# A new written issue order for an attention and feed-forward kernel on one core

## The chip, the core and the metric

The kernel runs on one core of a Trainium2 chip. A core has five engines, each with an instruction queue of its own that is worked off strictly in order: TensorE (PE; its weight loads are shown apart as PEld), VectorE (DVE), ScalarE (ACT), GpSimd (POOL) and SyncE (SP), which here only issues transfers. An instruction at the head of a queue that waits for another engine or for a transfer holds up everything behind it on that queue. The metric is the device time of one execution in microseconds (us).

## The reference

Causal-window attention with eight global keys, four sequences of 768 tokens, eight heads of 64; its output, 3072 x 512, goes through a feed-forward layer of 2048 with softplus in between:

```python
scores = scale * np.matmul(q, k.transpose(0, 1, 3, 2))
keep = is_global | is_local                      # the first 8 keys, and the last 96
scores = np.where(keep, scores + bias[None], -1000000000.0)
a = np.exp(scores - np.max(scores, axis=-1, keepdims=True))
a = a / (np.sum(a, axis=-1, keepdims=True) + 1e-09)
x = np.matmul(a, v)                              # then (B, S, H * D)
h = x @ w_in
g = np.maximum(h, 0.0) + np.log1p(np.exp(-np.abs(h)))
out = g @ w_out
```

The bias is minus a slope of the head times the distance; with only the last 96 and the first 8 keys kept, a block of 128 queries needs its own block of keys, the one before it, and the global keys, which are copied into unused rows of the block before.

## The kernel before, in words

**Tiling.** The 24 blocks of 128 queries (n = 0 to 23) are loaded in 12 units of two blocks. Two blocks make a group (g = 0 to 11) of 256 tokens for the feed-forward part. All of w_in and w_out stays on the chip in bf16. q, k, v and both weights arrive in float32 in a ring of 12 buffers (`raw`) and are cast to bf16 by DVE, ACT or POOL; a buffer is loaded again only when its casts are done.

**Operations.** Each step is an `op` with a name, and the names are what the order and this text speak of:

- `ldq`, `ldk`, `ldv` (lines 573 and 583): a unit's loads, 512 KB, for the first three units' q and k in two halves of 256 KB. `win0` to `win7` and `wout0` to `wout7` (614): the weights, 512 KB each.
- `castq`, `castk`, `castv` (634, 658): casts of a unit; `castv0.11` is unit 0, block 1, second half of the rows. `cin`, `cout` (616): casts of the weights.
- `trq`, `trk`: q and k transposed, for units 0 to 2 on PE (721) with the eviction `cpq`, `cpk` (728), later by a transposing transfer on SP (741).
- `sb`, `sc` (783 to 846): scores, for blocks 0 and 1 with the bias added by PE; for the others DVE adds it (`z`, 872). `ex` (806, 879): the exponential on ACT.
- `gk`, `gv` (754, 764): copies of the global keys and values into the block before.
- `pv` (898): probabilities times values, two halves of the heads; a column of ones gives the sums. `nm` (909, 910): a reciprocal and a multiplication on DVE.
- `xt`: the block transposed, for blocks 0 to 5 on PE (929) with the copy `xc` (934), later by a transfer on SP (941).
- `a{g}.{p}` (956): eight matmuls, 256 of the 2048 hidden columns of a group into one of two PSUM banks; p = 0 and 1 need `cin0` and `cin1`, p = 6 and 7 need `cin6` and `cin7`. `e` (971): exp on ACT. `ln` (982): log(1 + e) of two `a` steps at once.
- `b{g}.{ns}.{x}` (1003) for groups 0 to 2: products with w_out, and the eviction `oc` (1032). From group 3 on the product of the 2x2 blocks is made with seven multiplications in place of eight: `ws` (defined from line 391: sums of w_out blocks, done once), `ka{g}.{j}` (447: differences of the blocks of g), `b{g}.{j}` (512: eight matmuls), `oe` (477 to 498: the seven products put together). `st` (1035, 548): stores.
- `fill` (1116): 35 matmuls on a blank tile, on PE only; nothing reads them.

**Order and engines.** `Program` (from line 21) records every `op` with what it reads and writes. The string `ORDER` (lines 68 to 148) names all 1061 operations once, each with a letter for its engine; `PLACED` (149) splits it. `Program.op` takes the engine of an operation from there, and `in_order` issues the operations in the order of the string, after it has seen that every producer stands before its consumer. The string thus fixes each engine's queue completely, and, for those operations that may run on several engines, the engine:

```python
o.eng = self.placed[name]
...
for name in self.placed:
    o = self.ops[name]
    assert all(d.name in done for d in o.deps), (name, [d.name for d in o.deps if d.name not in done])
```

Waits between engines follow from reads and writes. Beyond those, the loads of units 3 to 11 wait for a given `a` step (`gates`), and the fillers follow each other. The numbers for durations and ranks in the calls of `op` play no part once the string is there.

Of the kernel before, what the change touches and what calls it, by code (L numbers as in the profile page):

```python
# [1271 lines left out]
```

## Time and profile before

| | us |
|---|---|
| median of 3 runs (lowest, highest) | 213.37 (212.76, 213.74) |
| the profiled execution | 213.29 |
| its span, first to last instruction | 211.4 |
| PE busy in it | 202.0 |
| ACT busy | 179.3 |
| DVE busy | 161.0 |
| POOL busy | 106.9 |
| granted TensorE clock, mean | 1.000 |

The views used: the page (busy time of each engine, groups of instructions by source line), the waits of an engine (who waited for whom: us in total, times, longest), the chain of work that ended last, the timeline (start, duration, engine, line, operation, what is written from what, and in brackets the idle time before it and what ended it), and the table of stretches (busy time of each engine between two moments). Rows are by source line; since both kernels issue each engine's operations in the order of the string, the n-th instruction of an engine is known by its name, and the texts below use the names.

By stage: until 19 us PE mostly runs fillers and the attention of the first blocks; from 24 us on it is busy nearly all the time; the last matmul of the program starts near 208, and four stores end the span. The 16 transfer engines are busy all the time until about 43 us (q, k, v of three units and both weights), and again in most of the time from 55 to 160.

### The profile page before, as it was taken

To read this page: it belongs to the slowest core of one execution; us is meant where nothing else is said; L and a number is where in the kernel's file an instruction comes from. 1 tells how busy PE (TensorE), PEld (TensorE's weight loads), DVE (VectorE), ACT (ScalarE), POOL (GpSimd) and SP (SyncE) were. 2 spreads that over 40 slices of the span, in tenths; PEclk is the share of its full clock that TensorE was granted. 3 is DMA by queue.
4 is the path that set the end of the run, shared out by engine and by line. 5 is a ranking of instruction groups with operands and counts; after the bars stand their busy time and mean duration, and the time that the engine had idled before them with its cause. 6 is when DMAs were issued, how large, how long until landed. Compare 5 with 4: busy or idle time off the path is not lost.

```text
span 211.4 us, 5443 instructions
## 1 busy us (share of the span) xinstructions
PE 202.0 (96%) x2176; PEld 161.8 (77%) x2187; DVE 161.0 (76%) x292; ACT 179.3 (85%) x260; POOL 106.9 (51%) x130
## 2 busy tenths in 40 slices
PE   7987999999999988999999999999999999999994
PEld 2564786666765766988988889889889889988883
DVE  4665888888779976988798898786868989624554
ACT  6886999999998899888899989998999899877510
POOL 4466541618769463565038794564465436061070
PEclk9999999999999999999999999999999999999999
DMA  5999999949996899976399988777595510300413
GB/s 202 348 329 321 395 387 353 333 119 211 290 225 154 206 256 177 323 187 126 103 232 185 242 213 175 175 181 174 134 210 130 179 22 3 101 3 0 152 77 122
DMA packets 69848, 40.98 MB, mean 194 GB/s; under 512 B 30144, under 2 KB 61376, under 8 KB 69824
## 3 DMA queue, kind: packets, MB, share of 16 engines
q1 hardware_dynamic: 69392, 39.99, 71.4%
q10 hardware_dynamic: 432, 0.66, 0.9%
q8 instruction: 17, 0.28, 0.6%
q14 instruction: 7, 0.06, 0.1%
HBM read 27.26 MB, written 6.29 MB: 159 GB/s over the span
## 4 chain that ended last, share of the span: by engine, by line
PE 64%; ACT 14%; DMA 11%; SPq 3%; issue 3%; POOL 2%; DVE 2%; DVEq 0%; POOLq 0%
PE h_ps L956 29%; PE o_ps L512 22%; DMA raw<-in_moe_w_out_dram 5%; ACT e L971 4%; PE s_ps L846 4%; DMA raw<-in_moe_w_in_dram 4%; PE x_ps L898 3%; PE o_ps L1003 3%; ACT g L982 3%; ACT pb L879 3%; DMA raw<-in_q_dram 3%; SPq L573 2%; PE x_ps L512 2%; POOL w_out_bf L616 1%; PE s_ps L512 1%
## 5 line engine op out<-in xcount | busy, mean ns | idle before, releaser
L956 PE MATMUL h_ps<-XT,w_in_bf 128*128 128x256 bf16 x768 | 94.5, 273 | 2.4 <-ACT XT L934 1.4
L956 PEld LDWEIGHTS <-w_in_bf 128*128 128x128 bf16 x768 | 72.9, 98 | 13.5 <-issue 1.2
L971 ACT ACTIVATE e<-h_ps 128x512 f32<-128x512 f32 x96 | 58.3, 635 | 11.4 <-PE h_ps L956 11.1
L982 ACT ACTIVATE g<-e 128x1024 bf16<-128x1024 f32 x48 | 49.8, 1056 | 0.8
L872 DVE TENSOR_TENSOR z<-s_ps,biasA 128x1024 f32<-128x1024 f32 x38 | 45.8, 1218 | 4.7 <-PE s_ps L846 2.6
L879 ACT ACTIVATE pb<-z 128x1024 bf16<-128x1024 f32 (+1 forms) x44 | 43.2, 993 | 0.2
L512 PEld LDWEIGHTS <-g 128*128 128x128 bf16 x288 | 27.6, 98 | 3.2
L658 POOL CAST kb<-raw 64x512 bf16<-64x512 f32 x25 | 17.1, 682 | 23.6 <-DMA raw<-in_k_dram 11.0
L447 POOL TENSOR_TENSOR g<-g 128x1024 bf16<-128x1024 bf16 x7 | 15.3, 2187 | 19.3 <-DVE raw L447 17.2
L658 POOL CAST vb<-raw 64x512 bf16<-64x512 f32 x30 | 19.2, 641 | 7.2 <-DMA raw<-in_v_dram 5.8
L512 PEld LDWEIGHTS <-raw 128*128 128x128 bf16 x216 | 20.7, 98 | 2.5
L764 POOL COPY vb<-vb 4x512 bf16<-4x512 bf16 x19 | 12.1, 638 | 19.0 <-PE x_ps L898 18.6
L512 PE MATMUL o_ps<-raw,raw 128*128 128x256 bf16 x168 | 20.8, 273 | 0.0
L898 PEld LDWEIGHTS <-pb 128*128 128x128 bf16 x352 | 16.6, 97 | 4.9 <-ACT pb L879 0.9
L447 DVE TENSOR_TENSOR raw<-g 128x1024 bf16<-128x1024 bf16 x21 | 15.1, 729 | 4.5 <-PE s_ps L512 2.4
L910 DVE TENSOR_TENSOR xs<-x_ps,rcp 128x256 bf16<-128x256 f32 x40 | 17.0, 425 | 1.4
L512 PE MATMUL o_ps<-raw,g 128*128 128x256 bf16 x144 | 18.0, 273 | 0.0
L447 POOL TENSOR_TENSOR raw<-g 128x1024 bf16<-128x1024 bf16 x6 | 13.1, 2184 | 7.8 <-ACT g L982 7.6
L898 PE MATMUL x_ps<-vb,pb 128*128 128x65 bf16 x304 | 15.9, 193 | 0.6 <-DVE xs L910 0.4
L1003 PE MATMUL o_ps<-w_out_bf,g 128*128 128x512 bf16 x59 | 15.4, 379 | 0.4 <-DVE vb L658 0.2
L909 DVE RECIPROCAL rcp<-x_ps 128x4 f32<-128x4 f32 x40 | 7.2, 180 | 10.6 <-PE x_ps L898 10.1
L1003 PEld LDWEIGHTS <-g 128*128 128x128 bf16 x96 | 8.6, 98 | 6.7 <-ACT g L982 0.3
(110 smaller groups left out, 247.4 us busy)
## 6 DMA issues: line engine op xcount, KB each, us to landing
raw<-in_v_dram SPq DMA_DIRECT2D x12, 512.0 KB, 4.8
out_dram<-osb SPq DMA_DIRECT2D x22, 256.0 KB, 2.9
raw<-in_q_dram SPq DMA_DIRECT2D x9, 512.0 KB, 4.3
raw<-in_k_dram SPq DMA_DIRECT2D x9, 512.0 KB, 4.6
raw<-in_moe_w_in_dram SPq DMA_DIRECT2D x8, 512.0 KB, 8.1
raw<-in_moe_w_out_dram SPq DMA_DIRECT2D x8, 512.0 KB, 9.8
raw<-in_k_dram SPq DMA_DIRECT2D x6, 256.0 KB, 5.6
raw<-in_q_dram SPq DMA_DIRECT2D x4, 256.0 KB, 4.9
```

The costliest lines, as they stand in the source:

```text
L447: (nc.vector if eng == "DVE" else nc.gpsimd).tensor_tensor(dst, a[0], b[0], ALU.subtract)
L512: nc.tensor.matmul(psum(j), lhs[:, f // 2, f % 2, :], w(f), start=(f == 0), stop=(f == 7))
L658: copy_on[eng](dst, src)
L764: copy_on[eng](vb_of(prev)[sl, :, 0:D], vb_of(first)[sl, :, 0:D])
L872: nc.vector.tensor_tensor(z, src, bias, ALU.add)
L879: nc.scalar.activation(pb[:, 0:nr, :].rearrange("p (y a) b -> p y (a b)", y=2), src, AF.Exp, scale=1.0 / root_d)
L898: nc.tensor.matmul(xv[:, h, :], pb[:, 4 * (h % 2) + 2 * part + h // 2 if lone else u_all * (2 * (h % 2) + h // 2) + u, :], vb_of(prev if u ...
L910: nc.vector.tensor_tensor(xs[:, 4 * part : 4 * part + 4, :], xv[:, :, 0:D], rcp[:][:, :, None].to_broadcast([P, 4, D]), ALU.mult,)
L956: last = nc.tensor.matmul(hv[:, j, :], w_in_bf[:, m, fb * P : fb * P + P], XT[g % NXG][:, m, :], start=(m == 0), stop=(m == NM - 1),)
L971: nc.scalar.activation(e[:, p % 2, :, :].rearrange("p j (b t r) -> p (j b) r t", b=2, r=2), hb[:].rearrange("p (a r t) -> p a r t", a=4, r=2),
L982: nc.scalar.activation(gt[:, 2 * p - 2 : 2 * p + 2, :].rearrange("p a t -> p (a t)"), e[:].rearrange("p a j t -> p (a j t)"), AF.Ln, bias=1.0,
L1003: nc.tensor.matmul(bank(key)[:, 0 : z - a], gt[:, fb, ns * P : ns * P + P], w_out_bf[:, fb, a:z], start=(fb == 0), stop=(fb == NFB - 1),)
```

## The change

Only the string `ORDER` is new. The set of operations, what each computes, the buffers, the PSUM banks and the dependencies are the same. 133 of the 1061 operations get another engine among those that they may run on; counts by engine:

| engine | operations before | after |
|---|---|---|
| PE | 324 | 324 |
| ACT | 263 | 251 |
| DVE | 233 | 243 |
| POOL | 124 | 126 |
| SP | 117 | 117 |

By kind: `ka` on POOL 13 before and 17 after, `ws` 6 and 5, `gv` 19 and 14, casts of q, k and v 66 and 67; on DVE `ka` 32 and 28, `ws` 14 and 15, `gv` 5 and 11, casts of q, k and v 18 and 26. Nearly every queue is reordered in many places; on PE the order within the last group stays. Since the new string has one line more, lines after it are numbered one higher in the profile of the changed kernel. The letters stand for PE (P), DVE (V), ACT (A), POOL (G) and SP (S). The diff, cut to the stretches that the prediction speaks of:

```diff
 ORDER = """
-blank:V ldq0.0:A iota:G ldk0.1:S fill0:P ldq0.1:A ldk0.0:S fill1:P dl1a:V fill2:P dl1c:V table:A ldq1.1:S dl0a:V
-fill3:P dl0b:V ldv0:S fill4:P dl0c:V ldk1.0:S dl1e:V fill5:P d0:G fill6:P ldq1.0:S biasTrue6:A d0e:V biasTrue2:A
-fill7:P biasFalse7:V biasFalse0:A biasFalse4:G fill8:P biasFalse3:A ldk1.1:S biasFalse1:A castq0.0:A fill9:P
-castk0.1:G ldv1:S biasTrue4:A ident:G biasFalse2:A biasTrue7:A castq0.1:V win1:S biasTrue5:A castk0.0:A biasFalse6:V
-trq0.0:P biasTrue1:V biasTrue0:A biasFalse5:V trk0.0:P biasTrue3:V cpq0.0:V fill10:P sb0.0:P cpk0.0:A cpq0.1:V
-fill11:P cpk0.1:A castv0.00:G fill12:P fill13:P castq1.1:V ones:G castk1.0:A sc0.0:P sb1.0:P castv0.01:G ex0.0:A
-sb1.1:P castq1.0:V ex0.1:A castv0.11:G sc1.0:P sc1.1:P ldq2.0:S ex1.0:A pv0.0:P fill14:P castk1.1:G win0:S nm0.0:V
-ex1.1:A ldq2.1:S castv0.10:G trq1.0:P fill15:P ldk2.0:S pv0.1:P cpq1.0:A pv1.1:P nm0.1:V trk1.0:P ldk2.1:S cpq1.1:A
-fill16:P nm1.1:V cin1:G pv1.0:P win2:S cpk1.1:A fill17:P xt0:P win3:S nm1.0:V cpk1.0:A fill18:P fill19:P win4:S
-castv1.11:G castv1.01:A fill20:P castv1.00:V sc2.0:P win5:S castq2.0:G xt1:P cin0:A win7:S fill21:P z2.0:V fill22:P
-fill23:P fill24:P win6:S gv4.1:G z2.1:V sc3.0:P castv1.10:A fill25:P gk4:G wout0:S xc1:V xc0:A fill26:P castq2.1:G
-sc3.1:P z3.0:V ex2.0:A a0.1:P castk2.1:G ex2.1:A castk2.0:G pv2.0:P a0.0:P nm2.0:V wout7:S trq2.0:P z3.1:V e0.0:A
-pv2.1:P cin2:G fill27:P ex3.0:A nm2.1:V trk2.0:P ex3.1:A cpq2.0:V fill28:P cin3:G xt2:P fill29:P fill30:P xc2:V
-fill31:P e0.1:A fill32:P wout1:S pv3.0:P cin4:G ln0.0:A fill33:P wout2:S a0.3:P nm3.0:V ldv2:S cpk2.0:A a0.2:P
-cin5:V e0.3:A cpk2.1:V pv3.1:P wout4:S a0.5:P e0.2:A cpq2.1:V cin7:G wout3:S ln0.1:A a0.4:P nm3.1:V e0.5:A sc4.0:P
-cin6:V e0.4:A xt3:P ln0.2:A a0.7:P wout6:S z4.1:V cout0:G a0.6:P e0.7:A xc3:V gv4.0:G z4.0:V fill34:P a1.1:P e0.6:A
...
-trq3:S nm5.0:V castk3.00:G a1.6:P castk3.01:A ws1.6:V castk3.10:A pv5.1:P castk3.11:A b0.0.10:P nm5.1:V b0.0.12:P
-gk6:A ln1.2:A trk3:S b0.1.10:P ws2.1:V b0.1.12:P ws0.7:V e1.6:A xt5:P b0.1.14:P e1.7:A ws1.3:V ws2.3:G b0.0.14:P
-ln1.3:A b1.0.8:P xc5:V ldv3:S ws2.7:V b1.0.10:P castv4.11:A a2.0:P ws2.4:G a2.1:P oc0.0.0:V e2.0:A oc0.1.0:A
...
-sc9.0:P trk5:S a3.0:P castv5.01:G z9.0:V pv8.0:P a3.1:P e3.0:A ldq6:S nm8.0:V st1.0.0:S ex9.0:A z9.1:V pv8.1:P
-a3.2:P e3.1:A gv9.0:G ln3.0:A nm8.1:V gv9.1:G ldk6:S ws3.1:G xt8:S pv9.0:P ex9.1:A a3.3:P nm9.0:V gk10:A e3.2:A
-pv9.1:P sc10.0:P e3.3:A nm9.1:V a3.4:P castq6.0:G ln3.1:A z10.0:V xt9:S a3.5:P gv10.1:G e3.4:A gv10.0:V ex10.0:A
-trq6:S a3.6:P z10.1:V e3.5:A b2.1.12:P castk6.11:G e3.6:A ldq7:S pv10.0:P ex10.1:A ldv6:S castk6.10:G a3.7:P
-nm10.0:V ln3.2:A a4.0:P castk6.01:V gk11:G oc2.1.0:V e3.7:A sc11.0:P castk6.00:V ln3.3:A pv10.1:P trk6:S a4.1:P
...
-b8.7:P e10.3:A z23.1:V ka9.2:G e10.2:A b8.6:P pv23.0:P ex23.1:A a10.4:P oe8.7:V nm23.0:V a10.5:P st8.0.0:S e10.4:A
-xt22:S ka9.7:V pv23.1:P b9.3:P e10.5:A nm23.1:V ln10.0:A b9.4:P ka9.1:V xt23:S ka9.5:V ln10.1:A a10.6:P oe9.a:V
...
-ln11.2:A b9.6:P ka10.1:V a11.7:P oe9.7:V a11.6:P ka10.7:V st9.0.0:S st8.1.0:S ka10.5:V b10.3:P st9.1.0:S e11.6:A
-e11.7:A b10.7:P ln11.3:A b10.6:P b10.4:P ka11.7:V b10.5:P ka11.5:V oe10.a:A ka11.6:V b10.2:P ka11.2:G b10.1:P
-oe10.b:V b11.3:P oe10.c:V b11.4:P oe10.1:V ka11.1:G oe10.7:V b11.5:P oe11.a:A st10.0.0:S b11.2:P st10.1.0:S b11.1:P
-oe11.b:V b11.7:P oe11.c:V b11.6:P oe11.1:V st11.0.1:S st11.1.0:S oe11.7:V oe11.6:V st11.0.0:A st11.1.1:S
+blank:V ldq0.0:A iota:G ldk0.0:S fill0:P table:A ldk0.1:S ldq0.1:A fill1:P dl0a:V dl0b:V fill2:P ldq1.1:S dl1a:V
+fill3:P dl0c:V ldv0:S dl1c:V fill4:P d0:G dl1e:V ldq1.0:S ident:G fill5:P biasTrue3:V biasTrue1:A biasTrue5:G
+fill6:P ldk1.1:S d0e:V fill7:P fill8:P ones:G ldk1.0:S biasFalse6:V fill9:P biasFalse5:A biasFalse1:V fill10:P
+biasTrue7:V win1:S fill11:P castk0.0:V fill12:P fill13:P biasFalse2:V castk0.1:A ldv1:S castq0.1:V castq0.0:A
+biasFalse3:V trk0.0:P biasTrue0:V biasFalse7:A biasTrue4:V biasFalse4:A trq0.0:P biasFalse0:V biasTrue2:A cpk0.0:V
+fill14:P fill15:P cpq0.0:A sb0.0:P cpk0.1:V cpq0.1:A fill16:P fill17:P castq1.1:V biasTrue6:A fill18:P sc0.0:P
+castv0.00:V ldq2.1:S castv0.01:V sb1.0:P ex0.0:A win0:S sb1.1:P ex0.1:A win2:S sc1.0:P castq1.0:G fill19:P sc1.1:P
+ex1.0:A castk1.1:G pv0.0:P fill20:P nm0.0:V castk1.0:G ex1.1:A trq1.0:P castv0.10:V pv0.1:P fill21:P cpq1.0:A
+nm0.1:V trk1.0:P cin1:G cpq1.1:A fill22:P cpk1.1:A castv0.11:G cpk1.0:A gk4:G pv1.1:P ldk2.1:S castv1.00:G xt0:P
+fill23:P nm1.1:V ldq2.0:S pv1.0:P castq2.1:G fill24:P sc2.0:P nm1.0:V ldk2.0:S castv1.11:G fill25:P z2.0:V win3:S
+xt1:P castv1.10:G cin0:A fill26:P win4:S fill27:P z2.1:V fill28:P castv1.01:G sc3.0:P win5:S xc1:A xc0:V sc3.1:P
+win6:S gv4.1:G z3.0:V ex2.1:A win7:S a0.1:P castk2.1:G ex2.0:A cin2:A pv2.0:P z3.1:V fill29:P fill30:P a0.0:P
+castk2.0:G ex3.0:A castq2.0:V trk2.0:P nm2.0:V e0.1:A fill31:P cin3:G fill32:P e0.0:A trq2.0:P ex3.1:A pv2.1:P
+a0.3:P wout1:S nm2.1:V cin4:G wout0:S cpq2.1:A cpk2.1:V xt2:P ldv2:S a0.2:P e0.3:A wout7:S xc2:V ln0.0:A cin5:V
+wout2:S pv3.0:P fill33:P fill34:P nm3.0:V wout4:S a0.5:P e0.2:A cin6:G wout3:S cpq2.0:V ln0.1:A pv3.1:P cpk2.0:V
+a0.4:P e0.5:A nm3.1:V cin7:G sc4.0:P e0.4:A xt3:P ln0.2:A a0.7:P z4.1:V cout1:G a0.6:P e0.7:A gv4.0:G xc3:V z4.0:V
...
+e1.7:A pv5.0:P gk6:G b0.0.10:P e1.4:A ws2.1:V castk3.01:G b0.0.12:P castk3.10:A nm5.0:V b0.1.10:P castk3.11:A
+b1.0.4:P castk3.00:V b1.0.6:P ws1.7:V ln1.2:A trk3:S pv5.1:P b0.1.12:P nm5.1:V a1.6:P gv6.1:A ws1.1:V b0.1.14:P
+ws1.3:V e1.6:A xt5:P b1.0.8:P ln1.3:A xc5:V ldv3:S b1.0.10:P ws1.6:V a2.1:P ws0.7:V oc0.1.0:A b0.0.14:P ws2.4:V
...
+b2.1.8:P castk5.11:G gk9:A ex8.0:A st1.0.0:S castv4.01:G sc9.0:P trk5:S a3.0:P z9.0:V pv8.0:P a3.1:P e3.0:A ldq6:S
+nm8.0:V ex9.0:A z9.1:V pv8.1:P a3.2:P e3.1:A gv9.1:G nm8.1:V ex9.1:A gv9.0:G a3.3:P ldk6:S ws3.1:V xt8:S e3.2:A
+pv9.0:P gk10:G ws3.4:G e3.3:A sc10.0:P nm9.0:V ln3.0:A pv9.1:P a3.4:P castv5.01:G nm9.1:V ln3.1:A castv5.10:G a3.5:P
+z10.0:V xt9:S e3.4:A castv5.00:G z10.1:V e3.5:A a3.6:P gv10.1:G ex10.0:A castk6.01:G a3.7:P gv10.0:V ldk7:S e3.6:A
+castk6.11:G castq6.0:V pv10.0:P ex10.1:A b2.1.12:P ldv7:S e3.7:A a4.0:P gk11:V castk6.10:V trq6:S ln3.2:A oc2.1.0:V
...
+ka9.6:G b8.7:P e10.3:A nm22.1:V e10.2:A xt22:S pv23.0:P b8.6:P ex23.1:A nm23.0:V a10.5:P ln10.0:A st7.1.0:S oe8.7:V
+ka9.7:G pv23.1:P st8.0.0:S b9.3:P ln10.1:A nm23.1:V a10.4:P e10.5:A xt23:S ka9.2:G ka9.5:V b9.4:P e10.4:A st8.1.0:S
...
+e11.0:A ka10.6:G oe9.b:V a11.2:P oe9.c:V e11.3:A b9.1:P e11.2:A ln11.0:A a11.5:P oe9.1:V ln11.1:A a11.4:P b9.7:P
+e11.4:A e11.5:A b9.6:P a11.7:P oe9.7:V a11.6:P ka10.7:V st9.1.0:S st9.0.0:S ka10.1:V ka10.5:G b10.7:P e11.6:A
+ka10.2:V ln11.2:A b10.6:P b10.3:P e11.7:A ln11.3:A b10.4:P b10.5:P ka11.6:V oe10.a:A ka11.7:V b10.2:P ka11.5:V
+b10.1:P oe10.b:V b11.3:P oe10.c:V ka11.2:V b11.4:P oe10.1:V b11.5:P oe11.a:A ka11.1:V b11.2:P oe10.7:V st10.1.0:S
+b11.1:P oe11.b:V st10.0.0:S b11.7:P oe11.c:V oe11.1:V b11.6:P st11.0.1:S st11.1.0:S oe11.7:V st11.0.0:A oe11.6:V
+st11.1.1:S
 """
```

97 lines of the change are left out of this document (48 added, 49 removed).

## The prediction

> **What bounds the kernel now.** I read the page first (span, busy shares), then the waits of the tensor engine (PE), then the order of time of the first 31 us, and last the two stretches later on where PE stands idle.
>
> ```profile
> span 211.4 us, 5443 instructions
> PE 202.0 (96%) x2176; PEld 161.8 (77%) x2187; DVE 161.0 (76%) x292; ACT 179.3 (85%) x260; POOL 106.9 (51%) x130
> ...
> PE h_ps L956 <- ACT XT L934: 1.4, 1, 1.4
> ...
> PE h_ps L956 <- ACT g L982: 0.8, 1, 0.8
> ...
> PE x_ps L898 <- DVE xs L910: 0.4, 1, 0.4
> ```
>
> PE is busy in 96% of the span, but that counts the 35 filler matmuls (op `fill`). The table of stretches says where the other 4% lie: PE is busy 36.00 of 36.00 us from 84 to 120, 40.00 of 40.00 from 120 to 160 and again from 160 to 200. From 84 us on nothing can be won before the tail; time can be won only ahead of it, and lost anywhere.
>
> ```profile
> 1.19 4.45 PE L1116 MATMUL x_ps<-blank 128*128 128x512 bf16 x10 [1.19 <-DVE blank L1055]
> ...
> 13.77 1.04 POOL L616 CAST w_in_bf<-raw 128x1024 bf16<-128x1024 f32 x1 [1.50 <-DMA raw<-in_moe_w_in_dram]
> ...
> 16.89 1.04 ACT L616 CAST w_in_bf<-raw 128x1024 bf16<-128x1024 f32 x1 [1.66 <-DMA raw<-in_moe_w_in_dram]
> ...
> 18.48 0.57 ACT L934 COPY XT<-h_ps 128x512 bf16<-128x512 bf16 x1
> ...
> 19.11 1.03 PE L956 MATMUL h_ps<-XT,w_in_bf 128*128 128x256 bf16 x8 [1.38 <-ACT XT L934]
> ```
>
> ```profile
> 27.57 0.69 DVE L616 CAST w_in_bf<-raw 128x1024 bf16<-128x1024 f32 x1
> ...
> 29.00 2.23 PE L956 MATMUL h_ps<-XT,w_in_bf 128*128 128x256 bf16 x17
> ...
> 74.81 0.46 PE L898 MATMUL x_ps<-vb,pb 128*128 128x65 bf16 x8 [0.40 <-DVE xs L910]
> ...
> 82.98 1.03 PE L956 MATMUL h_ps<-XT,w_in_bf 128*128 128x256 bf16 x8 [0.83 <-ACT g L982]
> ```
>
> The rows to see: the first feed-forward product (`a0.1`) starts at 19.11 because `cin0` (the cast of `win0`, 16.89) waited for its transfer and `xc0` stood behind it on ScalarE (ACT). The last cast of w_in (`cin6`, 27.57) again follows its landing, and `a0.7` starts at 29.00. So the transfers set the head.
>
> **The change part by part.** It holds the same 1061 operations; PE's 2187 weight loads are the same set. 133 operations change engine, the rest only place.
>
> *Loads and casts up to `a0.1`.* `win1` goes ahead of `ldv1` on SP's queue. Weight loads land 1.33 and 1.37 apart (casts at 20.55, 21.88, 23.25, each released by its DMA). In before, `q1.0` landed at 9.85, `k1.1` about 0.75 later, and `v1` and `win1` together by 13.77, so `v1` took about 1.8 and `win1` lands at 13.77 - 1.8 = 12.0. POOL then does `cin1` (1.04) and, new, `castv0.11` behind it (0.69, before done by 10.91): 13.7. On PE follow `pv1.1` (0.3), `xt0` (0.4), a filler and `pv1.0` (0.4): 14.85. VectorE (DVE) then `nm1.0` (0.64), `z2.0`, `z2.1` (0.70 each) and `xc0` (0.42, no longer on ACT): 17.1 to 17.3. ACT has `cin0` and `xc1`: `ldq2.0`, which waited for `castq1.0` until 10.46, no longer stands ahead of `win0`; `ldq2.1` does, and waits for `castq1.1` (8.32 in before), so `win0` is issued near 9.6 and not at 11.05. It lands at 13.75 (v1) + 0.7 + 1.36 = 15.8, or, if the slow stretch of the queue recurs (278 GB/s from 14 to 19, against 393 from 19 to 24), 1.2 later, as before: 17.0. With 1.04 for the cast and 0.57 for `xc1`, `a0.1` starts between 17.5 and 18.6, against 19.11: 0.5 to 1.6 sooner.
>
> *What is queued behind new waits there.* On SP `ldk2.1` now waits for `castv0.11` (13.7; before, `ldk2.0` waited for `castv0.10` until 12.26), and `ldq2.0`, `ldk2.0`, `win3` to `win7` stand behind it. `ldq2.0` needed 3.85 from issue to landing, so `k2.1` lands by 17.6, while `win0` and `win2` ahead of it keep the queue full until 17.1: 0.5 lost at most, inside the bound above. On ACT the table load (1.28) goes between `ldq0.0` and `ldq0.1`. No row shows a transfer issued behind a table load: either `ldq0.1` still goes at 1.40, or at 2.7 and lands 1.3 later (6.4 and not 5.12), which puts `sc0.0` near 9.2 (8.75 before).
>
> *Fillers.* 14 stand before the first transposes, 10 in before. Ten took 4.45, 0.43 each; later ones 0.21 to 0.27. Four more cost 0.85 to 1.7, so `trk0.0` starts at 6.5 to 7.3 where PE now reaches its first transpose at 5.78. Again `sc0.0` at 8.9 to 9.4. Both delays are covered: `sc2.0` could then go at about 15.2 through `ex1.1` and `cpk1.0`, and `z2.0` waits for `nm1.0` until 15.5 anyway; uncovered they would cost 0.1 to 0.4. [...]
>
> *Up to `a0.7`.* The same bytes stand before the last w_in load as before. It lands at 27.25 (`cin6` started 0.3 after that) with the slow stretch, or 1.2 sooner without: 26.05. But the last two casts, `cin6` and `cin7`, are now both on POOL (1.04, not 0.69): done by 27.1 to 28.3. PE's own line: `a0.5` at 24.8 at the earliest, `pv3.1`, `a0.4`, `sc4.0`, `xt3` behind it (2.8): 27.6. So `a0.7` starts at 27.6 to 28.4, against 29.00: -0.6 to -1.4. I take -0.9, the middle, as the queue's slow stretch is not explained by any row. `fill34`, which stood behind `a0.6`, is now spent earlier: -0.2.
>
> *29 to 84 us.* PE's idle time there is 0.2 + 0.1 + 0.8 + 1.1 = 2.2 (stretches 29:40, 40:55, 55:75, 75:84). ACT loses 12 operations (263 to 251): by row means its work from `a0.1` to `a3.7` falls from 55.6 to 53.1, on the engine that is busy 8.94 of 9.00 from 75 to 84. Yet most of the idle time is not ACT's. The 0.40 at 74.4 is two copies `gv9` on POOL in a row (0.61 each) after `pv8.1`; `pv9.0` now stands behind `a3.3` (0.87): gone, -0.4. But `pv9.1` then follows `pv9.0` with only `sc10.0` (0.55) between, and needs `nm9.0` (0.64 and its hand-overs): +0.3. The 0.83 at 82.15 ends when `xt9`, a transposing transfer, lands at 82.85; between `pv9.1` and `a4.0` PE has 0.5 less work, and one store of 0.7 fewer stands ahead of it: 0 (-0.7 to +0.5). The rest of the 2.2 may shrink by the ACT work taken off: -0.3. Together -0.4, from -2.2 to +2.
>
> *84 us to the end of PE.* Costed at nothing: PE has no gap there; the cover is the work between an operand's making and its use. 10 subtractions `ka` go from DVE to POOL and 6 back: 17 at 2.19 in place of 13. The shortest leads: 2.5 beyond its own time for `ka10.5`, 3.0 for `ka9.7`.
>
> *Tail.* `ka11.2` and `ka11.1` move from POOL (2.13 each) to DVE (0.69), between the `oe10` steps. `ka11.1` is done near 204.9 (205.19 before), `oe10.7` at 205.5 (204.18), and `oe11.b` starts at 205.75 after `b11.2`, as before. The two stores of group 10 go 1.4 later and still land before the last four. 0.
>
> **Sum** against the profiled execution's own 213.29 (span 211.40 and 1.89 around it; the median of the runs shown is 213.37): 213.29 - 0.9 - 0.2 - 0.4 = 211.8.
>
> **Rivals.** (1) *The middle opens too*: the slow stretch of the queue is gone (-1.4 - 0.2) and most of the 2.2 as well (-1.6): 210.1. For it: ACT's lighter load; against: the wait on `xt9` is a transfer's.
> (2) *The head's gain is hidden*: the slow stretch recurs and the two POOL casts come one after the other at the end, `a0.7` at 28.7, and `pv9.1` and `xt9` take what is left: 213.1. For it: nothing in the change gives the queue fewer bytes.
> (3) *POOL operands come late, slower*: from 84 to 200 every wait adds in full. A `ka` on POOL takes 1.5 more than on DVE; a subtraction that stands behind casts waiting for a load comes late by up to that. Two such in the dense part, with the head's -1.1 kept, give 213.29 - 1.1 + 3.0 = 215.2; from one late operand on the gain is spent. For it: four more of them, and copies `gv` in between; against: POOL is busy only 22.80 of 40 us from 120 to 160.
> (4) *DVE is held up by POOL's subtractions*: a `ka` on DVE took 0.69 at the median and up to 1.74, a `ws` up to 1.44, and the 32 and 14 of them together 4 us more than 0.69 each. With 17 in place of 13 on POOL that is about 1.2 more on an engine busy in 76% of the span: hidden, except ahead of `a2.1`, where `ws1.1`, `ws1.3` and `xc5` leave PE 0.5: +0.7, so 212.5. [...]
>
> **How the numbers follow.** Forecast 0.42 (211.8, its own range 211.0 to 212.6); (1) 0.14; (2) 0.16; (4) 0.10; (3) and its like 0.18. 0.5%, about what a measurement of this kernel tells from no change, is 1.07 us, so faster is below 212.3. Faster: (1), most of the forecast and a little of (4): 0.53; within: (2), the rest of the forecast and of (4): 0.28; slower: (3) and 0.01 of (2): 0.19. The range leaves out half of (1) below 210.0 and most of (3) above 214.5.
>
> **What would show it.** Right: `a0.1` at 17.5 to 18.6; first cast of w_in near 12.0; `a0.7` at 27.6 to 28.4; the gap before `pv9.0` gone, one of 0.3 before `pv9.1`; the transfer wait before `a4.0` still there; no PE gap from 84 to the tail; end of PE to end of span as before (211.4 - 208.3). Wrong: `castv0.11` later than 14.5, which delays `ldk2.1` and everything behind it on SP; a PE wait on a POOL operand in `L512` rows after 84 us; a PE busy share below 40.0 of 40 us there.

## The result and the profile after

The changed kernel takes 216.12 us (median of 4 runs, 215.38 to 217.23) against 213.56 us (4 runs, 212.76 to 214.66) for the kernel before in the same comparison: a ratio of 1.0105, 95% interval 1.0061 to 1.0148. It is slower by about 1%, clear of the interval; 211.8 was forecast. A second timing of the same kernel, in a later set of runs, gave 1.0147 (1.009 to 1.0205). The profiled execution of the changed kernel took 215.48 us, its span 213.4 us, at a mean granted clock of 0.998 (before: 213.29, 211.4, 1.000). The trace shows the full clock until 212.47 us, after TensorE's last matmul, so the clock is not the reason. From the last matmul's end to the end of the span both kernels need 3.1 us; the end of TensorE's work moved from 208.28 to 210.26 us.

The head of the page after (span; busy time, share and instructions of each engine):

```profile
span 213.4 us, 5451 instructions
...
PE 202.7 (95%) x2187; PEld 161.2 (76%) x2187; DVE 167.7 (79%) x302; ACT 172.6 (81%) x248; POOL 114.6 (54%) x132
```

ScalarE lost work, as the change said (179.3 before, 172.6 now), and GpSimd gained (106.9, 114.6). But VectorE is busy 6.7 us longer with ten instructions more. The extra lies in instructions that take longer: added up over all of VectorE's instructions, the time above the shortest one of the same form is 12.8 us in the trace before and 21.3 us after.

The waits of TensorE after (who waited for whom: us in total, times, longest):

```profile
PE x_ps L899 <- DVE xs L911: 1.3, 1, 1.3
...
PE h_ps L957 <- DVE w_in_bf L617: 0.6, 1, 0.6
PE o_ps L513 <- DVE osb L496: 0.6, 1, 0.6
PE o_ps L513 <- ACT osb L499: 0.5, 1, 0.5
...
PE o_ps L513 <- DVE osb L482: 0.4, 1, 0.4
...
PE s_ps L847 <- DVE z L873: 0.4, 1, 0.4
```

The longest is new (1.3 at `pv9.1`), and the `osb` and `z` rows are waits in a stretch where TensorE had none. The table of stretches of the two kernels says how much that is (length, then busy time and count for PE, PEld, DVE, ACT and POOL, granted clock, transfer share, GB/s). Before, then after:

```profile
29.00:84.00 55.00, 52.80 (x518) 36.41 (x525) 46.21 (x74) 51.92 (x75) 30.49 (x38) 1.00 0.94 239
84.00:200.00 116.00, 116.00 (x1327) 102.11 (x1327) 89.94 (x158) 103.30 (x145) 56.36 (x61) 1.00 0.62 150
```

```profile
29.00:84.00 55.00, 52.88 (x535) 36.73 (x534) 45.35 (x74) 48.56 (x69) 33.70 (x43) 1.00 0.93 243
84.00:200.00 116.00, 114.12 (x1300) 99.99 (x1295) 92.37 (x159) 99.72 (x142) 64.99 (x61) 1.00 0.67 147
```

From 84 to 200 us TensorE was busy 116.00 of 116.00 us and is now busy 114.12, so it waits 1.88 us where it had no wait. From 29 to 84 us the idle time is nearly unchanged (2.20, now 2.12): the gaps of 0.40 and 0.83 are gone, and the new 1.3 took their place. Compared at operations that have the same work on TensorE ahead of them, the changed kernel leads by 0.38 us up to `a5.6` (109.08 against 109.46), is 1.25 behind at `pv14.0` (115.84, 114.59) and 1.95 behind from `b6.2` (142.74, 140.79) to the end. So it loses 2.3 us in two short stretches.

**The four places.** The timeline of the changed kernel (start, duration, engine, line, operation; in brackets the idle time before it and what ended it) shows what stands beside and behind each. First `ws3.1` on VectorE, with the GpSimd work beside it and the wait at `pv9.1`:

```profile
73.80 1.27 POOL L765 COPY vb<-vb 4x512 bf16<-4x512 bf16 x2 [2.35 <-PE x_ps L899]
...
74.83 2.18 DVE L413 TENSOR_TENSOR raw<-raw,raw 128x512 bf16<-128x512 f32 x1
...
75.02 0.20 POOL L755 COPY kT<-kTa 128x32 bf16<-128x32 bf16 x1
...
75.19 1.27 POOL L413 TENSOR_TENSOR raw<-raw,raw 128x512 bf16<-128x512 f32 x1
...
77.62 0.40 PE L899 MATMUL x_ps<-vb,pb 128*128 128x65 bf16 x8 [1.31 <-DVE xs L911]
```

`ws3.1` takes 2.18 us where the form takes 0.69 alone; GpSimd runs three operations one behind the other in that time. `nm9.0`, which `pv9.1` needs, stands behind it on VectorE.

Then `gv14.1`, a copy of four rows, beside `ka4.1` and `castq8.0` on GpSimd, and the three waits that follow:

```profile
105.80 2.11 POOL L448 TENSOR_TENSOR raw<-g 128x1024 bf16<-128x1024 bf16 x1
107.87 1.03 POOL L635 CAST qb<-raw 128x1024 bf16<-128x1024 f32 x1
...
105.91 3.19 DVE L765 COPY vb<-vb 4x512 bf16<-4x512 bf16 x1
...
110.66 1.03 PE L513 MATMUL o_ps<-raw,raw 128*128 128x256 bf16 x8 [0.44 <-DVE osb L482]
...
112.93 0.62 PE L847 MATMUL s_ps<-qT,kT 64*128 64x128 bf16 x16 [0.36 <-DVE z L873]
114.10 1.03 PE L513 MATMUL o_ps<-raw,raw 128*128 128x256 bf16 x8 [0.55 <-DVE osb L496]
```

The copy starts 0.11 after `ka4.1` and ends 0.2 after `castq8.0`: it does not get through between the two. In the trace before, `gv14.1` took 0.64. `oe4.b`, `oe4.c`, `z14.1`, `z14.0` and `oe4.1` stand behind it on VectorE, and TensorE waits three times, 1.35 together.

Third, 138 us. On ScalarE `castk10.10` waits at the head of the queue for the load of k10; on VectorE `castk10.11` starts beside a subtraction on GpSimd:

```profile
138.23 2.12 POOL L448 TENSOR_TENSOR g<-g 128x1024 bf16<-128x1024 bf16 x1
...
138.72 0.62 ACT L659 CAST kb<-raw 64x512 bf16<-64x512 f32 x1 [0.99 <-DMA raw<-in_k_dram]
...
138.75 1.88 DVE L659 CAST kb<-raw 64x512 bf16<-64x512 f32 x1
...
139.36 0.63 ACT L880 ACTIVATE pb<-z 128x512 bf16<-128x512 f32 x1
139.90 1.04 ACT L983 ACTIVATE g<-e 128x1024 bf16<-128x1024 f32 x1
140.84 0.61 ACT L880 ACTIVATE pb<-z 128x512 bf16<-128x512 f32 x1
141.36 0.56 ACT L499 COPY osb<-o_ps 128x512 f32<-128x512 f32 x1
...
141.98 1.91 PE L513 MATMUL o_ps<-w_out_bf,g 128*128 128x256 bf16 x16 [0.53 <-ACT osb L499]
```

The `z` of the first ACTIVATE (`ex18.0`) had been ready since 137.34. The last copy (`oe6.a`) empties the PSUM bank that `b6.5` writes, and TensorE waits 0.53 for it. `castk10.11` takes 1.88 where 0.43 is usual; no wait of TensorE in this trace leads back to it.

Fourth, the head. GpSimd and SyncE of the changed kernel, and two of its stretches:

```profile
12.35 1.04 POOL L617 CAST w_in_bf<-raw 128x1024 bf16<-128x1024 f32 x1 [0.81 <-DMA raw<-in_moe_w_in_dram]
13.46 0.69 POOL L659 CAST vb<-raw 64x512 bf16<-64x512 f32 x1
...
9.56 1.11 SPq L615 DMA_DIRECT2D raw<-in_moe_w_in_dram  x2
14.17 0.54 SPq L574 DMA_DIRECT2D raw<-in_k_dram  x1
```

```profile
13.00:18.00 5.00, 4.51 (x67) 3.00 (x66) 4.40 (x11) 3.75 (x7) 4.64 (x9) 1.00 1.06 380
18.00:23.00 5.00, 4.47 (x49) 3.15 (x48) 3.15 (x7) 5.00 (x8) 2.47 (x4) 1.00 0.98 318
```

Between the issue of `win2` (done at 10.68) and that of `ldk2.1` (14.17) SyncE issues nothing for 3.5 us, because `ldk2.1` waits for `castv0.11`, which stands on GpSimd behind `cin1`, which waits for `win1`. Some four us after that hole's end the transfers run at 318 GB/s (18 to 23 us, after 380 from 13 to 18), and the last w_in lands at 27.93 (27.25 before). `a0.7` starts at 28.66 (29.00 before).

### The profile page after: what moved, and what is told of

Its sections match the earlier page's. It is cut to its first block, busy times and chain, and to the rows that moved or that the text cites. A ratio compares the mean times of both kernels' runs of the same rounds, so it can differ in the third digit from the quotient of the medians.

```text
span 213.4 us, 5451 instructions
## 1 busy us (share of the span) xinstructions
PE 202.7 (95%) x2187; PEld 161.2 (76%) x2187; DVE 167.7 (79%) x302; ACT 172.6 (81%) x248; POOL 114.6 (54%) x132
## 4 chain that ended last, share of the span: by engine, by line
PE 66%; DMA 14%; DVE 7%; SPq 4%; POOL 3%; issue 3%; ACT 1%; POOLq 0%; DVEq 0%; ACTq 0%
PE h_ps L957 30%; PE o_ps L513 18%; DMA raw<-in_k_dram 6%; PE o_ps L1004 5%; PE x_ps L899 4%; DMA raw<-in_moe_w_in_dram 4%; PE s_ps L1004 3%; DMA raw<-in_q_dram 3%; PE s_ps L847 3%; SPq L574 2%; DMA XT<-xs 2%; DVE z L873 2%; PE x_ps L513 1%; PE s_ps L513 1%; POOL vb L659 1%
## 5 line engine op out<-in xcount | busy, mean ns | idle before, releaser
L513 PEld LDWEIGHTS <-g 128*128 128x128 bf16 x288 | 27.5, 98 | 4.0 <-issue 0.7
L448 POOL TENSOR_TENSOR g<-g 128x1024 bf16<-128x1024 bf16 x9 | 19.8, 2203 | 15.8 <-DVE raw L448 15.7
L659 POOL CAST vb<-raw 64x512 bf16<-64x512 f32 x35 | 22.9, 657 | 5.7 <-DMA raw<-in_v_dram 4.3
L448 POOL TENSOR_TENSOR raw<-g 128x1024 bf16<-128x1024 bf16 x8 | 17.0, 2127 | 12.9 <-ACT g L983 11.6
L659 POOL CAST kb<-raw 64x512 bf16<-64x512 f32 x21 | 14.6, 694 | 8.5 <-DMA raw<-in_k_dram 8.0
L765 POOL COPY vb<-vb 4x512 bf16<-4x512 bf16 x14 | 8.5, 608 | 15.5 <-PE x_ps L899 14.9
L1004 PE MATMUL o_ps<-w_out_bf,g 128*128 128x512 bf16 x64 | 16.1, 380 | 0.0
L513 PE MATMUL o_ps<-w_out_bf,g 128*128 128x256 bf16 x112 | 13.9, 273 | 0.5 <-ACT osb L499 0.5
L448 DVE TENSOR_TENSOR raw<-g 128x1024 bf16<-128x1024 bf16 x19 | 13.0, 702 | 1.5 <-ACT g L983 1.4
```

The source lines that it names most:

```text
L448: (nc.vector if eng == "DVE" else nc.gpsimd).tensor_tensor(dst, a[0], b[0], ALU.subtract)
L513: nc.tensor.matmul(psum(j), lhs[:, f // 2, f % 2, :], w(f), start=(f == 0), stop=(f == 7))
L659: copy_on[eng](dst, src)
L765: copy_on[eng](vb_of(prev)[sl, :, 0:D], vb_of(first)[sl, :, 0:D])
L1004: nc.tensor.matmul(bank(key)[:, 0 : z - a], gt[:, fb, ns * P : ns * P + P], w_out_bf[:, fb, a:z], start=(fb == 0), stop=(fb == NFB - 1),)
```

## The experiments

Theory: the changed order loses in places that can be named (three operations on VectorE held beside GpSimd, one cast on ScalarE waiting for its load, one hole in the issue of loads). Rival: the changed order is longer as a whole, so that a wait taken away comes back further on. Ratios are to the kernel before, run on the same chip in the same set, with a 95% interval.

### Three operations moved away from where they stalled

```diff
-a3.3:P ldk6:S ws3.1:V xt8:S e3.2:A pv9.0:P gk10:G ws3.4:G e3.3:A
+a3.3:P ldk6:S xt8:S e3.2:A pv9.0:P gk10:G ws3.4:G ws3.1:G e3.3:A
...
-nm13.1:V gv14.0:G ln5.0:A gv14.1:V b4.2:P ka4.1:G
+nm13.1:V gv14.0:G ln5.0:A gv14.1:A b4.2:P ka4.1:G
...
-b6.4:P castk10.11:V xt17:S ln7.0:A sc19.0:P
+b6.4:P xt17:S ln7.0:A sc19.0:P
...
-nm18.0:V castk10.00:G ln7.2:A b6.2:P
+nm18.0:V castk10.00:G castk10.11:G ln7.2:A b6.2:P
```

By the theory the three waits of TensorE at `pv9.1` (1.31 us), from 110 to 115 us (1.35 together) and at `b6.5` (0.53) go with these edits.

> The new order with three operations taken out of the way of GpSimd: ws3.1 goes from VectorE to GpSimd, behind ws3.4; gv14.1 from VectorE to ScalarE at its place; castk10.11 from VectorE to GpSimd behind castk10.00. [...] Rival (the rest of the new order is too tight as a whole, and a wait that is removed comes back a few us later): the gaps reappear elsewhere with the same sum and the time stays at 215.0 to 215.8.

Measured: 215.42 us, 1.004 (1.0007 to 1.0073). The waits at 110 to 115 us are gone, that at `pv9.1` is 0.18, and VectorE's time above the shortest of each form falls from 21.3 to 15.8 us. `castk10.11` was the wrong one of the two casts: `b6.5` still waits 0.76, and `pv18.0` 0.44 ahead of it, since ScalarE stands 1.74 us at `castk10.10` (1.0 in the trace shown above). A new wait of 0.52 stands at 160 us, where `a9.1` waits for a transposing transfer. So from 84 to 200 us TensorE is still idle for 1.72, against 1.88, and the time lies where the rival had put it (the kernel before ran at 214.44 in that set). In this trace the head lost more than in the first one: 1.88 before `a0.3`, which waits for `cin3`, with `a0.7` at 30.20. Against the first timing of the changed order the ratio is 0.65% better, 1.4 us; the rest was not yet found.

### Only the head of the changed order

The operations up to `a1.1` in the changed order and on its engines, all others as in the kernel before. By the theory the loss lies behind this stretch and is not in this kernel, and `a0.7` starts as in the trace of the changed order (28.66). At the seam:

```diff
-xt3:P ln0.2:A a0.7:P wout6:S z4.1:V cout0:G a0.6:P e0.7:A xc3:V gv4.0:G z4.0:V fill34:P a1.1:P
+e0.4:A xt3:P ln0.2:A a0.7:P z4.1:V cout1:G a0.6:P e0.7:A gv4.0:G xc3:V z4.0:V
...
```

> The operations that the old order issues up to a1.1 stand in the new order's sequence and on its engines; everything after that is the old order. [...] The prediction's own sum for the head: -1.1, 212.2. Rival (the head's new order, with SP held behind ldk2.1, is what costs): 215 or more.

Measured: 218.75 us, 1.018 (1.0139 to 1.0221), the slowest of all, and inconclusive: the head loads w_out in another order than the rest uses it, and TensorE waits 2.57 at 35.8 us for a cast of it. Its profiled execution was 2.7 us longer than the median (221.48, clock 0.991), so that trace is used for the first 31 us alone: `a0.7` at 30.23.

### Only the rest of the changed order

The operations up to `a1.1` as in the kernel before, all others in the changed order; by the theory the idle time of TensorE that the change adds behind 29 us (1.8 us: 2.12 and 1.88 in place of 2.20) is still there:

```diff
-blank:V ldq0.0:A iota:G ldk0.0:S fill0:P table:A ldk0.1:S ldq0.1:A fill1:P dl0a:V dl0b:V fill2:P ldq1.1:S dl1a:V
+blank:V ldq0.0:A iota:G ldk0.1:S fill0:P ldq0.1:A ldk0.0:S fill1:P dl1a:V fill2:P dl1c:V table:A ldq1.1:S dl0a:V
...
```

> The operations that the new order issues up to a1.1 stand in the old order's sequence and on its engines; everything after that is the new order. [...] Rival (the head costs): level with before, 213.0 to 213.6.

Measured: 217.83 us, 1.013 (1.0091 to 1.017): as slow as the whole change. 1.013 is 2.8 us of the 214.44 that the kernel before took in that set, more than the 1.8 us that the theory counts on. The middle's waits are there without the new head: 1.2 at 77 us (0.72 of it at `sc10.0`, for a transposing transfer, and 0.50 at `pv9.1`, with `ws3.1` at 2.17), 1.34 from 111 to 115, 0.76 at 143; `gv14.1` takes 3.18. But the old head was late in this trace too: `ldq2.0` was issued at 11.52 (10.46 in the trace before) and `a0.7` starts at 30.14, so about 1.1 us of this trace's loss lies in the head. The run shows that the middle costs time by itself, not that it costs all of it; the head was open still.

### One GpSimd subtraction put on VectorE

```diff
-nm13.1:V gv14.0:G ln5.0:A gv14.1:V b4.2:P ka4.1:G
+nm13.1:V gv14.0:G ln5.0:A gv14.1:V b4.2:P ka4.1:V
```

By the theory `gv14.1`, no longer beside a subtraction of 2.11 us, is held by the cast behind it at most, and the three waits from 110 to 115 us (1.35) shrink.

> The new order with ka4.1 alone put from GpSimd on VectorE, at its place, so that GpSimd has no two-input subtraction beside gv14.1, which stays on VectorE. [...] Rival (a 4-row copy is simply slow on VectorE, or waits for something else): it still takes over 2.5 us and the gaps stay.

Measured, by a single timing: 216.68 us. `gv14.1` and, now behind it, `ka4.1` on VectorE:

```profile
107.75 1.14 DVE L765 COPY vb<-vb 4x512 bf16<-4x512 bf16 x1
108.91 1.00 DVE L448 TENSOR_TENSOR raw<-g 128x1024 bf16<-128x1024 bf16 x1
```

The copy itself is untouched, and takes 1.14 in place of 3.19; what went is its neighbour on GpSimd. It still ends with `castq8.0` (107.63 to 108.66). The waits from 110 to 115 shrink from 1.35 to 0.41, with VectorE doing 1.0 us more. The cause of this stall is shown, and the rival falls. For `ws3.1` and the casts the same cause is argued, from the GpSimd operations that ran beside them.

### The changed order again

> The new order as it is, beside the others on one chip. Both theories: 0.6 to 1.5% slower than before.

Measured: 218.24 us, 1.0147 (1.009 to 1.0205). The same waits at the same operations: 1.30 at `pv9.1`, 1.35 from 112 to 116, 0.76 at `b6.5`. The head is another: TensorE waits 1.70 for `cin3`, and `a0.7` starts at 30.74 where the first trace had 28.66. `castv0.11` ended at 14.88, later than the 14.5 that the prediction had named as the sign of a delay, and `ldk2.1` was issued at 14.91.

### A fourth cast moved, and a load later

To the three edits were added `castk10.10` behind `oe6.a`, and on SyncE the load of v5 and a store behind `xt7`; by the theory the waits at `pv18.0` and `b6.5` (0.44 and 0.76 with the three edits) go too:

```diff
-z18.1:V castk10.10:A a7.6:P nm17.1:V ex18.0:A b6.4:P
+z18.1:V a7.6:P nm17.1:V ex18.0:A b6.4:P
...
-st5.1.0:S oe6.a:A z19.0:V
+st5.1.0:S oe6.a:A castk10.10:A z19.0:V
...
-e2.7:A ldv5:S ws3.3:V pv7.0:P st1.1.0:S b2.0.4:P
+e2.7:A ws3.3:V pv7.0:P b2.0.4:P
...
-nm7.1:V castv4.11:G sc8.0:P xt7:S oc2.0.0:A
+nm7.1:V castv4.11:G sc8.0:P xt7:S ldv5:S st1.1.0:S oc2.0.0:A
```

> The new order with the three operations out of GpSimd's way as before, and two more places: castk10.10 on ScalarE moves from before ex18.0 to behind oe6.a, so that ScalarE does not stand waiting for ldk10 with the exponentials and the eviction oe6.a behind it; on SP ldv5 and st1.1.0 go behind the transposing transfers xt6 and xt7. [...] Rival (waits come back elsewhere): no faster than 0.4% slower than before.

Measured: 218.06 us, 1.0155 (1.0106 to 1.0204). A miss, made by the second edit. TensorE and GpSimd in its timeline:

```profile
76.16 0.40 PE L899 MATMUL x_ps<-vb,pb 128*128 128x65 bf16 x8 [2.35 <-POOL vb L659]
...
74.27 0.61 POOL L659 CAST vb<-raw 64x512 bf16<-64x512 f32 x1 [5.42 <-DMA raw<-in_v_dram]
```

`castv5.11` stands on GpSimd, waits 5.42 us for the load that now comes at 74.12, and holds up `castv4.01` behind it, whose rows had landed at 48.17 and which `pv8.0` needs. The four older waits were gone.

### The same with `castv0.11` ahead of `cin1`

```diff
-nm0.1:V trk1.0:P cin1:G cpq1.1:A fill22:P cpk1.1:A castv0.11:G cpk1.0:A gk4:G
+nm0.1:V trk1.0:P castv0.11:G cin1:G cpq1.1:A fill22:P cpk1.1:A cpk1.0:A gk4:G
```

> As the one with five places changed, and castv0.11 goes ahead of cin1 on GpSimd, so that ldk2.1 and all loads behind it on SP no longer wait for it until 14.1. If the hole in the transfer queue cost the head: ldk2.1 is issued near 12.5 and lands 0.7 sooner, the last w_in load and a0.7 come 0.5 to 0.8 sooner, and the time falls by 0.2 to 0.4%. If the transfer queue's slow stretch decides (it comes whatever the order), a0.7 and the time stay within 0.1%.

Measured: 216.06 us, 1.0081 (1.005 to 1.0113), so 2.0 us less than without this one edit, over twice what the theory had said. `ldk2.1` is issued at 13.29 (14.60), the wait of 1.85 for `cin3` is gone, and `a0.7` starts at 28.71 (30.56). A part of the gain is given back at `a0.1`, which now waits 1.69 for `xc0` on ScalarE and starts at 18.85 (18.08). The wait of 2.6 us at `pv8.0` is still there.

### The collision made in the kernel before

```diff
-e5.5:A nm13.1:V ln5.0:A b4.2:P ka4.1:V xt13:S castq8.0:V
+e5.5:A nm13.1:V ln5.0:A b4.2:P ka4.1:G gv14.1:V xt13:S castq8.0:V
...
-sc15.0:P gv14.1:V gv14.0:G trk8:S
+sc15.0:P gv14.0:G trk8:S
```

By the theory `gv14.1` is now held for as long as `ka4.1` beside it runs on GpSimd (2.11 us in the changed order).

> The old order with one collision put in: ka4.1 goes from VectorE to GpSimd at its place and gv14.1 (VectorE, 0.64 in the old order) right behind it. [...] Rival (gv14.1 was slow in the new order for another reason): it stays at 0.3 to 0.7.

Measured, by a single timing: 214.42 us. It missed its aim: GpSimd was free and ran `ka4.1` from 99.17 to 101.84, well before `gv14.1`, which started at 105.96 and took 0.29. It hit another operation instead: `ka4.6` on VectorE took 2.07 (0.68 before). TensorE did not notice, as it has no gap from 83 to 158 us. It does wait 0.67 at 159.35, for VectorE's `oe` ahead of `b7.1`, in a part of the order that is unchanged and has no wait in the trace before. The stall on VectorE is the same, and cost nothing here, where nothing on TensorE's path stands behind it.

### The four edits without the later load

`ws3.1`, `gv14.1` and `castk10.11` as in the first experiment, `castk10.10` behind `oe6.a`, `castv0.11` ahead of `cin1`; the load of v5 where the changed order has it. Five operations are moved; the texts call it the run, or the kernel, with four edits. Against the kernel of the last but one experiment:

```diff
-e2.7:A ws3.3:V pv7.0:P b2.0.4:P
+e2.7:A ldv5:S ws3.3:V pv7.0:P st1.1.0:S b2.0.4:P
...
-sc8.0:P xt7:S ldv5:S st1.1.0:S oc2.0.0:A
+sc8.0:P xt7:S oc2.0.0:A
```

> The changed order with four edits: ws3.1 to GpSimd behind ws3.4, gv14.1 to ScalarE, castk10.11 to GpSimd behind castk10.00 and castk10.10 behind oe6.a, and castv0.11 ahead of cin1; the load of v5 stays where the changed order has it. Theory (three stalls in the middle, made where VectorE stands beside GpSimd or ScalarE's queue stands behind a cast, and one at the head, where the load of k2 waits for castv0.11 behind cin1): all four stalls go and the 2.6 us at pv8.0 of the last attempt does not come; against 216.06 of that attempt some 2.0 us less (0.4 to 0.8 us of waits for xt7 and for sc8.0's transpose come back at 67 to 72 us), so 213.4 to 214.5 us, a ratio of 0.995 to 1.002 to the kernel before. Rival A (the stalls in the middle are refilled by later waits, the changed order is simply longer): 215.5 to 217, ratio 1.007 to 1.014. Rival B (the head's wait is not one thing but moves from trace to trace, so that putting castv0.11 first brings nothing): ratio about 1.004, as with the three edits alone.

Measured: 212.31 us, 0.9918 (0.9886 to 0.995): faster than the kernel before by 0.8%, and more than the theory had said. The stretches of its trace:

```profile
18.00:23.00 5.00, 4.30 (x45) 3.03 (x45) 2.27 (x6) 5.00 (x9) 2.70 (x4) 1.00 1.05 387
...
29.00:84.00 55.00, 53.33 (x542) 37.26 (x548) 45.02 (x76) 49.97 (x72) 33.28 (x43) 1.00 0.99 248
84.00:200.00 116.00, 116.00 (x1312) 101.99 (x1309) 89.06 (x158) 100.37 (x142) 65.46 (x62) 1.00 0.65 142
```

No gap from 84 to 200 us, 0.5 us less idle time from 29 to 84 than before, and transfers at 387 GB/s through the head. TensorE's work ends at 206.61 us (208.28 before, 210.26 in the changed order). The rival, that waits taken away come back, falls.

### The load late, without its victim

As the last, with the load of v5 and the store behind `xt7`, and `castv4.01` taken ahead of `castv5.11`:

```diff
-b2.1.4:P trq5:S z8.0:V ex8.1:A castv5.11:G b2.1.8:P castk5.11:G gk9:A ex8.0:A st1.0.0:S castv4.01:G sc9.0:P
+b2.1.4:P trq5:S z8.0:V ex8.1:A castv4.01:G castv5.11:G b2.1.8:P castk5.11:G gk9:A ex8.0:A st1.0.0:S sc9.0:P
```

> As the run with four edits, and on SyncE the load of v5 and the store st1.1.0 behind xt7, with castv4.01, whose rows landed 27 us earlier, taken ahead of castv5.11 on GpSimd. Theory (the 2.6 us at pv8.0 came from castv4.01 standing behind a cast that waited for the load of v5, and from nothing else): pv8.0 starts within 0.2 us of a3.0's end, the waits for xt7 and sc8.0's transpose shrink from about 0.4 us each to at most 0.2 each, so 0.2 to 0.8 us under the run with four edits: 212.8 to 214.2 us, ratio 0.991 to 1.000. Rival (the later load makes something else late: castv5.11 for pv10 or k6's casts): the same or slower than the run with four edits, with a wait of over 0.5 us on TensorE between 70 and 90 us.

Measured: 214.26 us, 1.0009 (0.9986 to 1.0031), 2 us more than without it. Half of the theory held: `pv8.0` starts right behind `a3.0`. The rival held for the rest. TensorE waits next at `sc10.0`:

```profile
77.08 0.62 PE L847 MATMUL s_ps<-qT,kT 64*128 64x128 bf16 x16 [1.60 <-DMA kT<-kb]
```

`castv5.11` waits for its load until 72.51, `castk5.11` stands behind it (done at 73.83), and the transposing transfer `trk5`, which needs that, lands at 77.03. `a4.0` waits 0.78 more, for another transposing transfer. A load moved back moved a whole chain.

### Only the cast at the head

The changed order with the one edit of `castv0.11`, as shown above.

> The changed order with one edit: castv0.11 ahead of cin1 on GpSimd. Theory (the load of k2 is issued some 0.9 us sooner, the queue of transfers has no hole, and cin3 or cin7 comes sooner): a0.7 ends 1.2 to 2.0 us sooner than in the changed order on the same chip (28.6 to 29.4 us against 30.5 to 30.7), the three stalls of the middle stay (about 1.3, 1.3 and 0.5 us), so 215.8 to 217.0 us, ratio 1.002 to 1.009. Rival (the two cases differed by chance, in where the transfers' slow stretch fell): no gain, 217.3 to 218.5, ratio 1.010 to 1.017, a0.7 at 30 us or later.

Measured: 215.30 us, 1.0046 (1.0019 to 1.0073), between 0.6% and 1.0% better than the two timings of the changed order. `a0.7` starts at 28.00 and ends at 29.20, inside the 28.6 to 29.4 of the theory; the waits of the middle are all there (1.30, 1.35, 0.76). The mechanism was met only in part: `ldk2.1` is issued at 13.88, 0.3 sooner than in the first trace of the changed order and not 0.9, because it also waits for `castv0.10`, and that cast took 1.29 us on VectorE beside `cin1` on GpSimd (0.43 in the kernel with four edits, where `win1` landed a quarter of a us later, so that `cin1` began after it).

### Only the middle

The kernel with four edits with `castv0.11` put back behind `cin1`:

```diff
-nm0.1:V trk1.0:P castv0.11:G cin1:G cpq1.1:A fill22:P cpk1.1:A cpk1.0:A gk4:G
+nm0.1:V trk1.0:P cin1:G cpq1.1:A fill22:P cpk1.1:A castv0.11:G cpk1.0:A gk4:G
```

> The run with four edits with its head put back: castv0.11 stands behind cin1 again as in the changed order, and only the middle differs (ws3.1, gv14.1, castk10.11 and castk10.10 away from where they stalled). Theory (middle and head each cost a share): the middle's edits take away 2.4 to 3.1 us of the changed order's 216.1 to 218.2, and the head's wait, worth 0.9 us by the issue of k2's load (14.17 against 13.06 us) and up to 2.0 us by the pair of runs that differed only in it, stays: 213.2 to 214.5 us, ratio 0.995 to 1.003. Rival A (the head's order is worth nothing, the middle is all): 212.0 to 212.9, ratio 0.990 to 0.994. Rival B (the cast of k10 on ScalarE is worth nothing, as the run with three edits had the other stalls off and was not faster): ratio 1.002 to 1.007.

Measured: 213.92 us, 0.9996 (0.9966 to 1.0025), inside the theory's span and outside both rivals'. Two stretches of its trace:

```profile
18.00:23.00 5.00, 4.31 (x45) 2.92 (x44) 3.15 (x7) 5.00 (x8) 1.65 (x3) 1.00 0.78 233
...
84.00:200.00 116.00, 116.00 (x1324) 101.66 (x1323) 89.87 (x161) 102.26 (x146) 66.02 (x64) 1.00 0.67 150
```

The middle is closed and the head open: `ldk2.1` issued at 14.34, 233 GB/s from 18 to 23 us, 1.71 of waiting for `cin3`, `a0.7` at 30.33, and 1.29 more of waiting for casts of w_out right behind it. With it the four cases stand side by side:

| ratio to before | `castv0.11` behind `cin1` | ahead of it |
|---|---|---|
| the middle as changed | 1.0105 and 1.0147 | 1.0046 |
| the middle's four operations moved | 0.9996 | 0.9918 |

The middle is worth 1.1 to 1.5% in one column and 1.3% in the other, the head 0.6 to 1.0% and 0.8%. Within the intervals, of 0.3 to 0.6% each way, the two add up, and together they are the whole difference between the changed order and the best one.

## Why the prediction was wrong

Step by step, in its own order.

*Loads and casts up to `a0.1`: right.* `a0.1` started at 17.71 (17.5 to 18.6 said), `win1` landed at 12.30 (12.0), `castv0.11` was done at 14.14 (13.7), short of the 14.5 named as a warning. In four other traces with this head it ended later, at 14.58 to 14.90.

*"0.5 lost at most" behind `ldk2.1`: the first step that failed.* The place and the chain were the right ones, and the size was not. The step took the transfers to be busy for as long as `win0` and `win2` had not landed. The trace shows a rate that falls from 380 GB/s to 318 from 18 to 23 us, and in the six other traces with this head to between 215 and 256. At 387 GB/s the bytes that 318 moves in five us take 4.1 us, those of 215 to 256 take 2.8 to 3.3: 0.9 to 2.2 us lost, not 0.5. Taking the cast ahead of `cin1` brought 1.7 to 2.0 us of time where the middle was the same (218.06 to 216.06, and 0.9996 to 0.9918).

*Up to `a0.7`, 27.6 to 28.4, so -0.9: failed in consequence.* 28.66 in the trace shown, and 30.20 to 30.74 in the six other traces with this head. The old head has 29.00, 28.70 and 30.14 in three. Without the hole it is 28.00 to 28.71 in four traces: two inside the range, two 0.3 above it. (The middle of -0.6 and -1.4 is -1.0, not -0.9.) The prediction left the "slow stretch" of the queue unexplained, and took the middle between its coming and its staying away. The traces point to the same thing as the wait that it had priced at 0.5: before, too, SyncE issues nothing from 7.03 to 10.46, and the rate falls from 385 GB/s (13 to 14 us) to 278 (14 to 19).

*Fillers and the table load: the times right, one of them by luck.* `ldq0.1` was issued at 1.44 while the table load ran from 1.41 to 2.69, so the load is not held by it; `trk0.0` came at 6.67 (6.5 to 7.3), `sc0.0` at 9.26 (8.9 to 9.4). But the 14 fillers were done at 5.88, where ten had taken until 5.64: four more cost 0.24, not 0.85 to 1.7, since the fillers from 4.4 us on came 0.22 apart and no longer 0.43. What held `trk0.0` for another 0.79 was `castk0.1` on ScalarE, done at 6.61.

*29 to 84 us, -0.4: the sum wrong, two of its terms too.* The 0.40 before `pv9.0` went, as said. The 0.83 before `a4.0`, said to stay, went too. The 0.3 before `pv9.1` became 1.31: its term counted `nm9.0` and the hand-overs, and not `ws3.1`, which the change puts ahead of `nm9.0` on VectorE and which took 2.18 beside GpSimd. Together the idle time stayed at 2.1 us. With `ws3.1` moved and the head closed it is 1.7, nearly the 1.8 of the prediction.

*"84 us to the end of PE. Costed at nothing": the step that lost the forecast.* The cover named was that of the moved subtractions' own results: none of them came late, and no wait on a GpSimd operand appeared. What came late were VectorE's and ScalarE's results, behind one operation that was held up. 1.88 us of waits there, 0 said. In all, TensorE's work was to end at 206.78 and ended at 210.26. Of these 3.48 us 0.66 were lost up to `a1.1` (0.44 won, 1.1 said), 0.45 from there to `a4.0` (nothing won, 0.4 said), and 2.37 behind `a4.0`, where the prediction had put nothing.

*Rival (4), VectorE held up by GpSimd, +0.7: the right mechanism, a seventh of its size and one place only.* It put about 1.2 us more on VectorE; the trace has 8.5 (12.8 to 21.3 above the shortest of each form). It went by the mean of the `ka` and `ws` in the trace before, where 16 of the 46 were beside a GpSimd operation (21 of 43 after), and it looked at subtractions alone, while a copy, a cast and a `ws` were hit. It looked for a path to TensorE in one place, `a2.1`, and the delays came out in two others. Rival (3) had the right shape of time, every wait past 84 us in full, and 215.2 us, with GpSimd's own results as its cause. Its price was near (215.48 in the profiled execution) for another reason.

*ScalarE's cast at the head of the queue: not in the prediction at all.* It costed ScalarE's lighter load as a gain of 0.3, and did not ask which of its operations wait for a load. The one that did cost 0.53 to 0.76 at `b6.5`, or 0.44 and 0.76 in the trace with three edits.

*Tail: right.* 3.1 us from the end of TensorE's work to the end of the span in both.

The terms of the forecast (-0.9, -0.2, -0.4) are what the order gives once `castv0.11`, `ws3.1`, `gv14.1`, `castk10.10` and `castk10.11` stand elsewhere: `a1.1` starts at 30.02 in place of 30.96, `a4.0` at 81.26 in place of 82.98, and from there on the kernel keeps its lead. That is the kernel with 212.31 us, not the changed one.

## What to carry to other kernels

In an issue order worked out from durations, look at each small operation that stands on a queue ahead of something on the critical path, and ask how long it can be held: by the operations that run beside it on GpSimd, or by a load that is not there yet. Short operations in such places cost their longest time here, not their usual one (`gv14.1` 3.19 us and not 0.29; `castk10.10` 0.62 and 0.99 of waiting ahead of it), and taking one cast ahead of another was worth 1.3 to 2.2 us of 214 here. A hole of over 3 us in the issue of loads showed up here as a low transfer rate some four us after its end (215 to 325 GB/s over five us, against 387 to 389 in the three runs of the changed head that issue `ldk2.1` by 13.29); before calling a slow stretch of transfers bad luck, look at when they were issued.
